# A fixed order on three engines up to the second cell of a fused attention and two-layer kernel

## Chip, cores and metric

The kernel runs on one core of a Trainium2 chip. The metric is the device time of one execution in microseconds (us). The engines are TensorE (PE, matrix products into PSUM), VectorE (DVE), ScalarE (ACT), GpSimd (POOL) and SyncE (SP, whose queue issues all the DMAs here). Each engine works through its own queue in order and waits on the others by semaphores.

## What is computed

A Nyström attention over 4 batches of 8 heads (sequence 576, head size 64, 32 landmarks) feeds two layers, one multiplicative and one with a mish activation. Cut to what matters:

```python
q_lm, k_lm = (mean over 18 neighbours of q, of k)       # 32 landmarks per head
A, Bm, C = sm(q, k_lm), sm(q_lm, k_lm), sm(q_lm, k)     # sm: softmax of the scaled scores
Z = Bm.T / (norms of Bm)
for _ in range(6):
    Z = 2 * Z - Z @ Bm @ Z
x = A @ Z @ C @ v                                       # 2304 tokens x 512
x = ((x @ w_a) * (x @ w_b)) @ w_out                     # width 1536
h = x @ w_in2
out = (h * tanh(softplus(h))) @ w_out2                  # width 2048
```

## The kernel before, in words

All products of the two layers run as three products of rounded halves (a high part and the rest, fp32r), and the fp32 weights first go through a bitwise conversion: `to_f32` (L310) is one ACT instruction (L317) and four DVE instructions on a 128x512 piece (L320, L323, L324, L325). The weights of the first layer come in 36 such units (`Units`, L336): for each of three parts of the width there are eight units for w_a and w_b (two groups of four, which land in a tile `wab`) and four for w_out (`wo1_unit`, which also splits the piece into high and rest, tile `wo`).

Attention runs per batch, in steps of `attention` (L118): `kl`, `ql` sum keys and queries to landmarks; `sB`, `BB` make the small score matrix and its start for the inverse; six `NS` steps iterate the inverse (tile `rz`), each a PE step of small matmuls, then an ACT copy and a DVE add; the last also makes `zd`; `sC0`, `sC1` are the scores of all keys (tile `E`), `ET0`, `ET1` their transposes, `U` the product with the values, `M` joins U and the inverse (tile `mt`); `A0`, `A1` score the two halves of the queries and `A0n`, `A1n` normalise them (tile `at`, a high part from ACT and the rest from POOL, L288).

The first layer is cut into 12 **cells** of (batch, part of the width), and each cell into 8 **slots**. `emit_bm` (L404) folds M into the first layer's weights (a **fold**, two per cell: PE matmuls `ps_bm<-wab,mt`, ACT high part, DVE rest, tile `bm`). A slot (`emit_ab`, L430) is twelve matmuls `ps_ab<-at,bm` in two halves, an ACT copy `ta`, a DVE product `tg` (L437), an ACT high part and a POOL rest (tile `g`, 9 buffers). `emit_o1` (L447) is the product with w_out: 8 **o1** pieces per cell, each twelve matmuls `ps_o<-g,wo` over four `g` tiles and four `wo` tiles.

The order: PE and ACT instructions written through `Written` (L37) stay in the order of the code until L603; those of DVE are placed by a scheduler, except a few that are pinned. Up to there the code is a string of steps of batch 0 (L593), with `u` for a whole conversion unit and digits for warming matmuls on the identity. After that the 96 slots run in a loop (L634); work that has a due time in slots lies in a list `todo` (L617): the steps of batch 1 between slots 0.5 and 5.5, four w_out units from slot 2, the second part's twelve units from slot 6 to 18, and so on; and each slot emits one waiting o1 piece between its halves (`between`, L652), two in slots 7 and 8. From L603 on the scheduler orders PE and ACT too.

Of the kernel before, what the change touches and what calls it, by code (L numbers as in the profile page):

```python
# [17 lines left out]
LM = 32  # L18
# [13 lines left out]
def nystrom_moe_kernel(ctx: ExitStack, tc: tile.TileContext, q, k, v, w_a, w_b, w_out1, w_in2, w_out2, out):  # L32
    nc = tc.nc
    NT = B * S
    ve, gp = nc.vector, nc.gpsimd

    class Written:  # L37
# [7 lines left out]
        def __getattr__(self, name):  # L45
            f = getattr(self.engine, name)

            def call(*a, **kw):
                i = f(*a, **kw)  # L49
                if Written.on:  # L50
                    tc.keep_in_program_order(i)
                return i

            return call

    ac, pe = Written(nc.scalar), Written(nc.tensor)
# [8 lines left out]
    ps = ctx.enter_context(tc.tile_pool(name="ps", bufs=1, space=PSUM))  # L65

    def bank(tag):
        return ps.tile([128, 512], F32, tag=tag, bufs=2, name=f"ps_{tag}")

    def pair_bank(tag):  # L70
        return ps.tile([128, 2, 512], F32, tag=tag, bufs=1, name=f"ps_{tag}")
# [22 lines left out]
    def load_qk(ap, b):  # L94
        out = []
        for src, nm, tag in ((k, "kt", "kv"), (q, "qt", "qt")):
            t = ap.tile([128, 4, S], F32, tag=tag, bufs=1, name=nm)
            nc.sync.dma_start(out=t.rearrange("p j s -> p (j s)"), in_=src[b])
# [18 lines left out]

    def attention(ap, b, kt, qt, vt0=None):  # L118
# [3 lines left out]
        wheel = [0]  # L122
# [4 lines left out]
        def pair():  # L127
            wheel[0] += 1
            return pair_bank("bm" if first and wheel[0] % 2 else "at")

        def lm_sum(src, nm):
            x[nm] = sm([128, 4, LM], nm)
            for j in range(0, 4, 2):
# [15 lines left out]
        def sB():  # L149
            p = pair()  # L150
            tile4(p, lambda o, rows, j: (o[:, 0:32], x["ql"][rows, j, :], x["kl"][rows, j, :]))
            st = x["st"] = sm([128, 2, 8], "stB")
# [3 lines left out]
            ac.activation(eb, eb, AF.Exp, scale=SC_B)  # L156
            ve.tensor_reduce(out=st[:, :, 2], in_=eb, axis=AX, op=ALU.add)
# [7 lines left out]
        def BB():  # L165

            st, bc = x["st"], x["bc"]
            p = pair()
            for c in range(2):
# [3 lines left out]
                for h in range(4):  # L173
                    r = slice(32 * h, 32 * h + 32)
                    pe.matmul(p[r, c, 64:96], bc[r, c, 1], bc[r, c, 1], start=True, stop=True)
            ve.tensor_reduce(out=st[:, :, 0:2], in_=p[:, :, 0:64].rearrange("p c (a l) -> p c a l", a=2), axis=AX, op=ALU.max)
# [10 lines left out]
        def NS():  # L187
# [4 lines left out]
            p = pair()  # L192
            nx = x["rz"] = sm([128, 2, 2, LM], "rz", 2)
            for c in range(2):
                for h in range(4):
# [4 lines left out]
                    )  # L200
            if not lo:
                ac.activation(nx[:, :, 0], p[:, :, 0:32], AF.Copy)
            ve.tensor_tensor(nx[:, :, 1], p[:, :, 32:64], rz[:, :, 1], op=ALU.add)
            if lo:
                zd = x["zd"] = sm([128, 2, 4, LM], "zd")
                for c in range(2):
                    (ve if first else gp).tensor_tensor(zd[:, c], bd3, nx[:, c, 1:2].to_broadcast([128, 4, LM]), op=ALU.mult)

        def sC(r):
            if r == 0:  # L210
                x["sc"], x["pc"] = sm([128, 4, 2], "stC"), []
            sc, p = x["sc"], pair_bank("bm" if r else "at")
            x["pc"].append(p)
            tile4(p, lambda o, rows, j: (o[:, 0:288], x["ql"][rows, j, :], kt[rows, j, 288 * r:288 * r + 288]))
            ve.tensor_reduce(out=sc[:, r], in_=p[:, :, 0:288], axis=AX, op=ALU.max)
            if r == 0:
                return
            ve.tensor_tensor(sc[:, 2], sc[:, 0], sc[:, 1], op=ALU.max)
# [3 lines left out]
            for r, p in enumerate(x.pop("pc")):  # L222
                for c in range(2):
                    ac.activation(E[:, c, 288 * r:288 * r + 288], p[:, c, 0:288], AF.Exp, bias=sc[:, 3, c:c + 1], scale=SC_A)

        def e_T(c):
            if c == 0:
                x["ET"] = sm([128, 2, 5, 128], "ET")
            p = pair()
# [5 lines left out]
            ac.activation(ET[0:64, 4], p[0:64, 1, 0:128], AF.Copy)  # L235

        def Uv():
            p = pair()
            for c in range(2):
                for i in range(5):  # L240
                    r = slice(0, min(128, S - 128 * i))
                    for j in range(4):
# [4 lines left out]
                        if (c, i, j) == (0, 0, 0):  # L247
                            tc.keep_in_program_order(ins)
# [6 lines left out]
        def M():  # L255
            p = pair()
# [145 lines left out]
    bm = {}  # L402
# [466 lines left out]
```

## Time and profile before

| | |
|---|---|
| median of 3 runs | 863.75 us (861.7 to 863.79) |
| the profiled execution's own time | 862.38 us |
| its span | 860.6 us |
| mean granted TensorE clock, share of full speed | 0.969 |
| busy in the span: PE, DVE, ACT, POOL | 94%, 64%, 40%, 18% |
| bytes moved by DMA | 180.87 MB |

A row of a timeline or of the chain of waits starts with the start in us and the length in us. A group of instructions names line, engine, operation, tile written <- tiles read, shapes and a count, then busy time and the mean length in ns. Behind a bar or in brackets stands the idle time before the instructions and who ended it. A PE "busy" includes modelled ends, so a PE that is busy all the time is not necessarily at its peak.

### The profile page before, as it was taken

The numbers are of one execution on the slowest core, as the hardware profiler recorded it, in microseconds if no ns is written. First come the engines' busy times: TensorE is split into PE (matmuls) and PEld (weight loads), VectorE is DVE, ScalarE is ACT, GpSimd is POOL, SyncE is SP. The second block draws the span as 40 slices with busy tenths as digits, with TensorE's granted clock in tenths as the row PEclk, the third lists the DMA queues.
The fourth block names the chain that finished last, engine by engine and source line by source line (L and its number), as shares of the span: only waits on it lengthen the run. The fifth ranks groups of instructions, "written<-read, shape, count | busy, mean of one in ns | idle before, by whom it ended". The sixth has DMA issues, their size and how long they took to land.

```text
span 860.6 us, 14629 instructions
## 1 busy us (share of the span) xinstructions
PE 805.4 (94%) x5830; PEld 696.0 (81%) x5830; DVE 553.3 (64%) x1024; ACT 346.1 (40%) x686; POOL 157.0 (18%) x147
## 2 busy tenths in 40 slices
PE   4767799999999999999898899999999999999998
PEld 3445578887897797887798799898989888998986
DVE  7787868888375379787996667858533347432433
ACT  3234436435332464353444545445323235332332
POOL 0022211222122133121226433521000000000000
PEclk9778699999999999999999999999999999999999
DMA  9532746649543816877576976789755446655502
GB/s 356 239 117 99 254 151 200 226 152 319 197 156 114 308 34 221 292 226 266 175 235 250 346 249 216 269 293 339 296 185 201 158 180 219 212 204 194 184 1 75
DMA packets 47605, 180.87 MB, mean 210 GB/s; under 512 B 4144, under 2 KB 12336, under 8 KB 37936
## 3 DMA queue, kind: packets, MB, share of 16 engines
q1 hardware_dynamic: 47536, 179.93, 58.8%
q8 instruction: 46, 0.75, 0.3%
q14 instruction: 23, 0.19, 0.1%
HBM read 126.44 MB, written 53.48 MB: 209 GB/s over the span
## 4 chain that ended last, share of the span: by engine, by line
PE 79%; DVE 12%; DMA 5%; issue 2%; ACT 1%; POOL 1%; SPq 0%; DVEq 0%; ACTq 0%
PE ps_ab L49 34%; PE ps_o L49 22%; PE ps_bm L49 13%; PE ps_at L49 10%; DVE f L324 1%; DMA wi2d<-f 1%; DVE f L325 1%; DVE f L320 1%; DMA qt<-in_q_dram 1%; DVE tg L437 1%; DMA kt<-in_k_dram 1%; DVE f L323 1%; DMA wo2d<-f 1%; DMA xq<-x2d 1%; DVE ql L138 1%
## 5 line engine op out<-in xcount | busy, mean ns | idle before, releaser
L49 PE MATMUL ps_ab<-xc,wc 128*128 128x384 f32 x1008 | 201.9, 339 | 2.6 <-ACT m L49 2.1
L49 PEld LDWEIGHTS ps_ab<-xc,wc 128*128 128x128 f32 x1008 | 181.6, 189 | 15.1 <-ACT m L49 2.3
L49 PE MATMUL ps_ab<-at,bm 128*128 128x288 f32 x1152 | 187.1, 303 | 6.9 <-DVE tg L437 4.3
L49 PEld LDWEIGHTS ps_ab<-at,bm 128*128 128x128 f32 x1152 | 161.3, 190 | 37.6 <-issue 9.8
L49 PE MATMUL ps_o<-g,wo 128*128 128x288 f32 x1152 | 182.2, 300 | 10.1 <-ACT wo L49 4.3
L49 PEld LDWEIGHTS ps_o<-g,wo 128*128 128x128 f32 x1152 | 162.6, 190 | 23.9 <-issue 7.3
L334 POOL TENSOR_TENSOR g<-tg,g 128x288 fp32r<-128x288 f32 x96 | 88.1, 918 | 283.6 <-ACT g L49 283.6
L49 ACT ACTIVATE m<-c 128x384 f32<-128x384 f32 x96 | 50.4, 525 | 185.5 <-DVE c L759 185.5
L49 PE MATMUL ps_bm<-wo,g 128*128 128x512 f32 x288 | 94.1, 394 | 0.3 <-ACT g L49 0.3
L49 PE MATMUL ps_at<-wo,g 128*128 128x512 f32 x288 | 83.3, 393 | 0.0
L49 PE MATMUL ps_o<-wo,g 128*128 128x512 f32 x288 | 79.4, 393 | 0.0
L49 ACT ACTIVATE g<-tg 128x288 fp32r<-128x288 f32 x96 | 42.6, 444 | 86.7 <-DVE tg L437 86.6
L334 DVE TENSOR_TENSOR g<-m,g 128x384 fp32r<-128x384 f32 x96 | 60.7, 633 | 25.8 <-ACT g L49 25.7
L437 DVE TENSOR_TENSOR tg<-ps_ab,ta 128x288 f32<-128x288 f32 x96 | 43.4, 452 | 30.3 <-PE ps_ab L49 24.3
L49 PEld LDWEIGHTS ps_at<-wo,g 128*128 128x128 f32 x288 | 53.9, 188 | 10.3
L49 PEld LDWEIGHTS ps_o<-wo,g 128*128 128x128 f32 x288 | 53.6, 188 | 8.9
L49 PEld LDWEIGHTS ps_bm<-wo,g 128*128 128x128 f32 x288 | 53.4, 187 | 7.0 <-ACT g L49 0.6
L49 ACT ACTIVATE ta<-ps_ab 128x288 f32<-128x288 f32 x96 | 38.9, 405 | 44.0 <-PE ps_ab L49 43.6
L49 ACT ACTIVATE g<-m 128x384 fp32r<-128x384 f32 x96 | 50.6, 527 | 2.9
L759 DVE TENSOR_TENSOR c<-ps_ab,m 128x384 f32<-128x384 f32 x24 | 13.4, 557 | 51.8 <-PE ps_ab L49 51.8
L49 PE MATMUL ps_bm<-wab,mt 64*32 64x512 f32 x384 | 42.2, 636 | 1.2 <-ACT mt L49 0.7
L759 DVE TENSOR_TENSOR u2s<-ps_ab,m 128x384 f32<-128x384 f32 x24 | 13.4, 557 | 44.6 <-PE ps_ab L49 44.2
(144 smaller groups left out, 832.8 us busy)
## 6 DMA issues: line engine op xcount, KB each, us to landing
wc<-wcd SPq DMA_DIRECT2D x16, 1792.0 KB, 7.3
wo<-wod SPq DMA_DIRECT2D x16, 1024.0 KB, 4.8
stg<-in_moe_w_out_dram SPq DMA_DIRECT2D x28, 512.0 KB, 4.5
wcd<-wc SPq DMA_DIRECT2D x8, 1792.0 KB, 7.2
wab<-wabd SPq DMA_DIRECT2D x10, 1024.0 KB, 6.5
stg<-in_moe_w_in_dram SPq DMA_DIRECT2D x16, 512.0 KB, 4.9
wod<-wo SPq DMA_DIRECT2D x8, 1024.0 KB, 6.5
stg<-in_moe_w_a_dram SPq DMA_DIRECT2D x12, 512.0 KB, 5.5
```

What stands on the lines that cost most here:

```text
L49: i = f(*a, **kw)
L138: i = ve.tensor_reduce(out=x[nm][:, j:j + 2], in_=src[:, j:j + 2].rearrange("p j (t k) -> p j t k", k=BLK), axis=AX, op=ALU.add,)
L320: i = ve.tensor_scalar(dst, dst, F32_TINY, F32_HUGE, op0=ALU.max, op1=ALU.min)
L323: ve.tensor_scalar(du, du, 3, 0x3FFFFFFF, op0=ALU.logical_shift_left, op1=ALU.bitwise_and)
L324: ve.scalar_tensor_tensor(du, hi, 0xC0000000, du, op0=ALU.bitwise_and, op1=ALU.bitwise_or)
L325: ve.scalar_tensor_tensor(du, lo, 29, du, op0=ALU.logical_shift_right, op1=ALU.bitwise_or)
L334: lo_eng.tensor_tensor(dst_lo, src, dst_hi.bitcast(F32), op=ALU.subtract)
L437: ve.tensor_tensor(tg, pb[:, 0:288], ta, op=ALU.mult)
L759: ve.tensor_tensor(t, p[:, 0:TB], other, op=ALU.add)
```

## The change

All three engines get a written order up to the end of the first cell. The VectorE handle is wrapped like those of ScalarE and TensorE (`ve = Written(nc.vector)`). Every attention step and every conversion becomes a generator that yields at its handovers, and two strings, `FIRST` (batch 0) and `SECOND` (cell (0, 0) with batch 1, marked +), place the pieces one by one; a "." is one piece of a conversion. The DVE work of conversion units 5 to 8, which the scheduler had put ahead of the first fold's rest, moves into `SECOND`. All eight slots of cell (0, 0) stand in `SECOND`; all eight o1 pieces of that cell are deferred: they start after slot 9, and slots 10 to 17 emit two pieces each. `A1` and `A1n` of batch 1 and the four w_out units come at slots 8 to 10, the second part's units at slots 10 to 18. The first three `g` tiles get buffers of their own (12 in all), `qt` gets two buffers, so that batch 1's queries load at the start; batch 0's keys and queries load in halves. PSUM is laid out in a first pool with a third pair of banks (`p3`). The rest of the first `at` tile of batch 0 and `zd` of batch 1 move from POOL to DVE. The warming matmuls in the string go from 25 to 17.

```diff
-    ve, gp = nc.vector, nc.gpsimd
+    gp = nc.gpsimd
...
-    ac, pe = Written(nc.scalar), Written(nc.tensor)
+    ac, pe, ve = Written(nc.scalar), Written(nc.tensor), Written(nc.vector)
...
+        out, step = [], 4 if b else 2
+        for src, nm, tag, bufs in ((k, "kt", "kv", 1), (q, "qt", "qt", 2)):
+            t = ap.tile([128, 4, S], F32, tag=tag, bufs=bufs, name=nm)
+            for j in range(0, 4, step):
+                nc.sync.dma_start(out=t[:, j:j + step].rearrange("p j s -> p (j s)"), in_=src[b][:, S * j:S * (j + step)])
...
+    PAIRS0 = {"sC0": "p3", "ET0": "bm", "ET1": "p3", "A0": "bm", "U": "p3"}
+    PAIRS1 = {"ET0": "bm", "ET1": "bm"}
...
-                    (ve if first else gp).tensor_tensor(zd[:, c], bd3, nx[:, c, 1:2].to_broadcast([128, 4, LM]), op=ALU.mult)
+                    (ve if b < 2 else gp).tensor_tensor(zd[:, c], bd3, nx[:, c, 1:2].to_broadcast([128, 4, LM]), op=ALU.mult)
...
-            gp.tensor_tensor(at[:, 1], af, at[:, 0].bitcast(F32), op=ALU.subtract)
+            (ve if (b, r) == (0, 0) else gp).tensor_tensor(at[:, 1], af, at[:, 0].bitcast(F32), op=ALU.subtract)
...
+    FIRST = """
+        kl kl ql ql . sB sC0 sC1 4 sB . sB BB 3 sC0 BB NS 2 . NS NS 2 . NS NS 2 sC1 NS NS 2 sC1 . sC1 NS NS 1 . sC1 NS NS 1 . NS
+        ET0 ET1 . . U A0 . . A0 . . U A0 M . . . . f0 A1 A0n A0n A0n f0
+    """
+    SECOND = """
+        s0 s0 A1 A1 s0 s1 s1 +kl A1n A1n s1 A1n +kl s2 s2 +ql s2 +ql s3 s3 +sC0 . s3 +sC0 +sC1 . +sC1 +sC1 +sC1 +sC1
+        +sB . +sB . . +sB +BB . . +BB +NS . +NS +NS . +NS +NS . +NS +ET0 +NS . . +NS +ET1 +NS . . +NS +NS . . +NS
+        f1 +U f1 s4 s4 +U +M F s4 s5 s5 F +A0 s5 s6 s6 +A0 +A0 s6 s7 s7 +A0n +A0n s7 +A0n
+    """
...
+        if gpool is None:
+            t = p1.tile([128, 2, 288], F32R, tag="g", bufs=9, name="g1")
+        else:
+            t = gpool.tile([128, 2, 288], F32R, tag="gx", bufs=3, name="g1")
...
-    u0.prefetch()
-    run0 = attention(ap, 0, kt, qt, load_v(ap, 0))
+    u0.prefetch(4)
+    vt0 = load_v(ap, 0)
+    u0.prefetch(8)
+    run0 = attention(ap, 0, kt, qt, vt0)
+    run1 = attention(ap, 1, *load_qk(ap, 1))
+    u0.prefetch(10)
...
-    for e in 'kl ql sB sC0 sC1 u 7 BB 8 NS ET0 1 NS ET1 u NS 2 A0 NS u 2 A0n NS U u 3 NS 2 M u'.split():
...
+    part["."] = weights()
+    part["f0"] = fold(0, 0)
+    go(FIRST, run0)
...
+    part["f1"], part["F"] = fold(0, 1), fold(1, 0)
+    for n in range(8):
+        part[f"s{n}"] = ab(0, n // 4, n // 2 % 2, n % 2, ap if n < 3 else None)
+    go(SECOND, run0)
     Written.on = False
...
-    for w, t0, t1 in ((1, 6, 18), (2, 18, 34)):
+    for w, t0, t1 in ((1, 10, 18), (2, 18, 34)):
...
-        todo.append((2 + 0.9 * n, 99, u0.step))
+        todo.append((8 + 0.5 * n, 99, u0.step))
...
-            if o1q:
+            if o1q and si > 9:
                 emit_o1(*o1q[0], i)
                 if i == 1:
                     o1q.pop(0)
-            if si in (7, 8) and i == 1:
-                for part in range(2):
-                    emit_o1(*o1q[0], part)
+            if si in range(10, 18) and i == 1:
+                for h in range(2):
+                    emit_o1(*o1q[0], h)
                 o1q.pop(0)
```

Three places of the resulting order. VectorE, batch 0, around the start of the `NS` steps: `rz` is the iterate, `wab` a conversion of w_a and w_b, `stC` the maximum of the key scores. Before:

```order
L182 TENSOR_TENSOR rz<-ps_at,stB 128x2x32
L184 TENSOR_TENSOR rz<-bc,stB 128x2x32
L324 SCALAR_TENSOR_TENSOR wab<-stg,wab 128x2x256
L320 TENSOR_SCALAR wab<-wab 128x2x256
L325 SCALAR_TENSOR_TENSOR wab<-stg,wab 128x2x256
L183 TENSOR_TENSOR rz<-ist,rz 128x2x32
L325 SCALAR_TENSOR_TENSOR wab<-stg,wab 128x2x256
L320 TENSOR_SCALAR wab<-wab 128x2x256
L323 TENSOR_SCALAR wab<-wab 128x2x256
L320 TENSOR_SCALAR wab<-wab 128x2x256
L203 TENSOR_TENSOR rz<-ps_bm,rz 128x2x32
```

After:

```order
L56 TENSOR_TENSOR rz<-ps_at,stB 128x2x32
L56 TENSOR_TENSOR rz<-ist,rz 128x2x32
L56 TENSOR_TENSOR rz<-bc,stB 128x2x32
L56 TENSOR_SCALAR wab<-wab 128x2x256
L56 TENSOR_TENSOR rz<-ps_at,rz 128x2x32
L56 SCALAR_TENSOR_TENSOR wab<-stg,wab 128x2x256
L56 TENSOR_TENSOR rz<-ps_at,rz 128x2x32
L56 TENSOR_REDUCE stC<-ps_bm 128x2
L56 TENSOR_TENSOR rz<-ps_at,rz 128x2x32
L56 TENSOR_TENSOR stC<-stC 128x2
L56 TENSOR_SCALAR stC<-stC 128x2
L56 SCALAR_TENSOR_TENSOR wab<-stg,wab 128x2x256
```

Between two steps of `rz` stand up to eight conversion instructions before and about one now.

TensorE, from cell (0, 0)'s first slots into batch 1's attention (`ps_ab<-at,bm` are slots, 12 matmuls each; the small ones are steps sB, sC, BB). Before:

```order
L49 MATMUL ps_ab<-at,bm 128x288 x24
L49 MATMUL ps_at<-kl,ql 32x32 x2
L49 MATMUL ps_bm<-kt,ql 32x288 x2
L49 MATMUL ps_at<-kl,ql 32x32 x6
L49 MATMUL ps_bm<-kt,ql 32x288 x6
L49 MATMUL ps_at<-kt,ql 32x288 x8
L49 MATMUL ps_ab<-at,bm 128x288 x12
L49 MATMUL ps_at<-bc,ones 32x64 x4
L49 MATMUL ps_at<-bc 32x32 x4
L49 MATMUL ps_at<-bc,ones 32x64 x4
L49 MATMUL ps_at<-bc 32x32 x4
L49 MATMUL ps_bm<-wab,mt 32x512 x8
```

After:

```order
L56 MATMUL ps_ab<-at,bm 128x288 x48
L56 MATMUL ps_at<-kt,ql 32x288 x8
L56 MATMUL ps_bm<-kt,ql 32x288 x8
L56 MATMUL ps_at<-kl,ql 32x32 x8
L56 MATMUL ps_at<-bc,ones 32x64 x4
L56 MATMUL ps_at<-bc 32x32 x4
L56 MATMUL ps_at<-bc,ones 32x64 x4
L56 MATMUL ps_at<-bc 32x32 x4
L56 MATMUL ps_at<-rz 32x64 x24
L56 MATMUL ps_bm<-ident,E 128x128 x4
```

Four slots now stand in a row, and batch 1's steps follow without a slot between them.

TensorE, around the o1 pieces that need the fourth w_out tile (`wo_947` before, `wo_1104` after; these two are the same tile). Before:

```order
L49 MATMUL ps_bm<-wab,mt 32x512 x8
L49 MATMUL ps_o_1036<-g_1004,wo_947 128x288 x2
L49 MATMUL ps_o_1079<-g_1004,wo_947 128x288 x2
L49 MATMUL ps_o_1036<-g_1004,wo_947 128x288
L49 MATMUL ps_o_1079<-g_1004,wo_947 128x288
L49 MATMUL ps_ab<-at,bm 128x288 x4
L49 MATMUL ps_o_1105<-g_564,wo_705 128x288 x3
```

After:

```order
L56 MATMUL ps_o_1131<-g_894,wo_1080 128x288
L56 MATMUL ps_o_1165<-g_894,wo_1080 128x288
L56 MATMUL ps_ab<-at,bm 128x288 x6
L56 MATMUL ps_o_1131<-g_926,wo_1104 128x288 x2
L56 MATMUL ps_o_1165<-g_926,wo_1104 128x288 x2
L56 MATMUL ps_o_1131<-g_926,wo_1104 128x288
L56 MATMUL ps_o_1165<-g_926,wo_1104 128x288
L56 MATMUL ps_ab<-at,bm 128x288 x7
L56 MATMUL ps_o_1195<-g_533,wo_998 128x288 x3
```

The place comes after 8 slots and three folds before, and after 15 slots and four folds now.

## Rows read from the trace of the kernel before

**Rows 1.** The page: the span, and busy time of each engine.
```profile
span 860.6 us, 14629 instructions
...
PE 805.4 (94%) x5830; PEld 696.0 (81%) x5830; DVE 553.3 (64%) x1024; ACT 346.1 (40%) x686; POOL 157.0 (18%) x147
```

**Rows 2.** Busy time of each engine by stage, with granted clock; columns in the first line.
```profile
core 0: us, PE busy (x) PEld busy (x) DVE busy (x) ACT busy (x) POOL busy (x), PEclk, DMA share, GB/s
0.00:10.00 10.00, 1.21 (x6) 1.24 (x7) 4.16 (x4) 1.28 (x1) 1.33 (x12) 1.00 0.82 309
10.00:30.00 20.00, 13.76 (x182) 10.67 (x181) 19.93 (x55) 9.23 (x20) 0.00 (x0) 0.82 1.04 405
30.00:45.40 15.40, 11.27 (x199) 7.05 (x198) 8.12 (x22) 2.89 (x6) 1.40 (x1) 0.79 0.32 115
45.40:60.00 14.60, 8.88 (x76) 5.42 (x76) 14.29 (x29) 3.12 (x7) 3.53 (x3) 0.78 0.31 112
60.00:78.00 18.00, 16.30 (x194) 12.95 (x193) 11.44 (x27) 10.89 (x27) 5.47 (x6) 0.90 0.27 100
78.00:99.00 21.00, 11.26 (x176) 6.40 (x176) 16.83 (x38) 7.40 (x14) 4.47 (x4) 0.57 0.65 228
...
101.50:156.00 54.50, 54.50 (x398) 43.93 (x397) 41.58 (x69) 27.48 (x59) 9.13 (x10) 1.00 0.56 180
```

**Rows 3.** The chain that ended last, 0 to 170 us: start, length, what.
```profile
0.75 0.38 SPq L98
1.19 7.61 DMA qt<-in_q_dram
8.82 2.61 DVE ql L138 x2
...
44.21 1.23 DVE bm L334
...
104.50 1.02 PE ps_bm L49 x16
...
146.43 1.59 PE ps_ab L49 x12
```

**Rows 4.** Timeline: the last conversion before o1 runs freely, the first free o1, the next slot.
```profile
98.40 0.69 DVE L334 TENSOR_TENSOR wo<-f,wo 128x512 fp32r<-128x512 f32 x1 [1.92 <-ACT wo L49]
...
99.79 1.70 PE L49 MATMUL ps_o<-g,wo 128*128 128x288 f32 x6
```

**Rows 5.** DVE's groups, 0 to 110 us: busy us, mean ns of one, idle before.
```profile
L324 DVE SCALAR_TENSOR_TENSOR wab<-stg,wab 128x512 uint32<-128x512 uint32 x11 | 8.1, 733 | 0.1
...
L334 DVE TENSOR_TENSOR bm<-ps_bm,bm 128x1024 fp32r<-128x1024 f32 x4 | 4.9, 1223 | 6.0 <-ACT bm L49 6.0
...
L437 DVE TENSOR_TENSOR tg<-ps_ab,ta 128x288 f32<-128x288 f32 x9 | 4.1, 453 | 3.0 <-ACT ta L49 2.1 <-PE ps_ab L49 0.9
...
L282 DVE TENSOR_TENSOR sa<-sa,stA 128x576 f32<-128x576 f32 x4 | 3.0, 758 | 0.1
...
L207 DVE TENSOR_TENSOR zd<-bdm,rz 128x128 f32<-128x128 f32 x2 | 0.5, 289 | 0.1
```

**Rows 6.** Timeline: the first NS matmuls, one step's ACT and DVE part, matmuls at lower clock.
```profile
24.12 0.43 PE L49 MATMUL ps_bm<-rz 32*32 32x64 f32 x16 [1.91 <-DVE rz L183]
...
66.15 0.23 ACT L49 ACTIVATE rz<-ps_at 128x64 f32<-128x64 f32 x1 [0.71 <-PE ps_at L49]
...
66.64 0.21 DVE L203 TENSOR_TENSOR rz<-ps_at,rz 128x64 f32<-128x64 f32 x1
...
31.26 0.65 PE L49 MATMUL ps_bm<-rz 32*32 32x64 f32 x16
```

**Rows 7.** Timeline: a fold's ACT part; slots, product U and a fold at the lower clock.
```profile
43.15 1.02 ACT L49 ACTIVATE bm<-ps_bm 128x1024 fp32r<-128x1024 f32 x1 [1.25 <-PE ps_bm L49]
...
58.63 2.77 PE L49 MATMUL ps_ab<-at,bm 128*128 128x288 f32 x10 [0.68 <-POOL at L288]
...
86.84 2.87 PE L49 MATMUL ps_at<-vt,ET 128*32 128x65 f32 x80 [1.62 <-issue]
...
97.90 1.96 PE L49 MATMUL ps_bm<-wab,mt 64*32 64x512 f32 x16 [0.37 <-ACT mt L49]
```

More of the change, by code (lines that the diff above doesn't have):

```diff
@@ L294, in attention, with run @@
         }
-        return lambda name: steps[name]()
+        part = {}
+        def run(name, whole=True):
+            g = part.pop(name, None) or steps[name]()
+            for _ in g:
+                if not whole:
+                    part[name] = g
+                    return
+        return run
+    FIRST = """
[7 more added lines that the diff above has]
+    """
     def stage(src, shape, early):
@@ L413, in emit_bm @@
         t = main.tile([128, 2, 2, 512], F32R, tag="bm", bufs=3, name="bm")
-        split(t[:, 0], t[:, 1], p, ac, ve)
+        ac.activation(t[:, 0], p, AF.Copy)
+        yield
+        ve.tensor_tensor(t[:, 1], p, t[:, 0].bitcast(F32), op=ALU.subtract)
         bm[b, g] = t
+    def emit_bm(b, g):
+        for _ in fold(b, g):
+            pass
     g1 = {}
@@ L590, in fill, with weights, go @@
             pe.matmul(p[:, 0:128], ident, ident, start=True, stop=True)
[L592 to L602 removed]
+    def weights():
+        gs = []
+        for n in range(8):
+            u0.n += 1
+            u0.prefetch()
+            gs.append(u0.units[n][2](u0.st[n]))
+        next(gs[0])
+        yield
+        for n, g in enumerate(gs):
+            for i, _ in enumerate(g):
+                if i == 2 and n < 7:
+                    next(gs[n + 1])
+                yield
+            yield
+    part = {}
+    def go(text, run):
+        for e in text.split():
+            if e.isdigit():
+                fill(int(e))
+            elif e[0] == "+":
+                run1(e[1:], False)
+            elif e in part:
+                next(part[e], None)
+            else:
+                run(e, False)
+    part["."] = weights()
+    part["f0"] = fold(0, 0)
+    go(FIRST, run0)
+    p3 = None
+    ps_ctx.close()
+    ps.append(ctx.enter_context(tc.tile_pool(name="ps", bufs=1, space=PSUM, reuse_waits="tile")))
+    part["f1"], part["F"] = fold(0, 1), fold(1, 0)
+    for n in range(8):
+        part[f"s{n}"] = ab(0, n // 4, n // 2 % 2, n % 2, ap if n < 3 else None)
+    go(SECOND, run0)
     Written.on = False
[L604 to L605 removed]
     CELLS = [(b, w) for w in range(3) for b in range(2)] + [(2, 0), (2, 1), (3, 0), (3, 1), (2, 2), (3, 2)]
```

144 lines of the change are left out of this document (78 added, 66 removed).

## The prediction, made before the changed kernel ran

> **What bounds the kernel now.** I read the page first: over the 860.6 us PE is busy for 94% and DVE for 64% [rows 1], so the end of the kernel is set by PE, and a change of order can only gain where PE lacks work. The stages show where that is [rows 2]. From 101.5 to 156 us PE is busy for all 54.5 us. Ahead of that it is not: the clock falls to 0.57 of full speed between 78 and 99 us, and PE's records there are stretched. In these first 99 us DVE is the engine with the work: 19.93 us of 20 between 10 and 30, 14.29 of 14.60 between 45.4 and 60, 16.83 of 21 between 78 and 99; in all 4.16 + 19.93 + 8.12 + 14.29 + 11.44 + 16.83 = 74.8 us busy and 24.2 idle. The chain of waits says the same in its first part: queries from DMA, the landmark sums on DVE, later the rest of the first fold, which ends at 45.4 us [rows 3]. PE becomes free of DVE when the fourth w_out tile is split, at 98.40 + 0.69 = 99.1 us, and the last o1 matmuls that needed it end at 99.79 + 1.70 = 101.5 us [rows 4]. So I ask how much PE work is done when DVE has finished that same tile in the new order, and when that is.
>
> **PE's side of the comparison.** In the new order the place behind the fourth w_out tile comes after 15 slots and 4 folds; before, after 8 slots and 3 folds; the o1 matmuls done are the same 24. Seven slots at 1.59 us and one fold at 1.02 [rows 3] are 12.1 us of dense PE work. The old kernel, dense from 101.5 on, has done as much at 101.5 + 12.1 = 113.6 us. Everything that lets the new order reach the place before 113.6 us is gain; PE's work behind it is the same.
>
> **DVE's work up to there.** Removed: nothing. Added ahead of the place: six products tg at 0.453, two rests of folds at 1.223; moved from POOL: one rest of at (128x576; no row on DVE, by the nearest of that shape, sa, 0.758) and two zd at 0.289, which overlap to 0.5 [rows 5]. That is 2.7 + 2.4 + 0.8 + 0.5 = 6.4 us on the 74.8, or 81.2 us. So DVE has more to do, not less; the gain must come from this work doing PE more good, and from less idle time. The new order by itself I walked with the durations of the groups, each stage's sum times 0.92, because neighbouring instructions overlap: along the old order the durations of all the groups of that view add up to 81.1 us, and the stages show 74.8 [rows 2].
>
> Start: the keys and queries come in halves. Before, the queries land at 8.8 us and their sums end at 11.4 [rows 3]. With halves each sum runs behind its own half, and only the last, 1.3 us, is left after 8.8: 10.1 us. Two more issues on SP's queue, 0.38 us each [rows 3], come ahead of the weights, behind the sums of the keys; I cost them at nothing, and uncovered they would cost 0.8.
>
> 10.1 to 23.1: sB, BB, six NS. Before, the first NS matmul started at 24.1 us [rows 6], because up to eight conversion instructions stood between the small ones. Now it starts at 15.0. One NS step is PE 0.43 us, ACT 0.23, and DVE 0.21 after ACT [rows 6], with handovers 1.12 us; at the lower clock PE takes 0.65 and the step 1.34. A conversion piece (at most 0.73 [rows 5]) fits in the 0.9 us in which DVE waits for the next step. Six steps with one delay of 0.7, where ACT makes E first, end at 22.6, zd at 23.1. DVE is busy 8.9 of these 13 us.
>
> 23.1 to 40.9: transposes, U, A0, M, first fold. Here DVE waits for ACT to copy the transposes before it may convert unit three (1.5 us), for the scores A0 behind U on PE (1.3), and at the end for ACT's high part of at. Busy 12.5 of 17.8. The rest of the first fold ends at 40.9, against 45.4 [rows 3]: 4.5 us earlier, but with four conversions fewer behind it, about 8 us of DVE work that is still to come.
>
> 40.9 to 71: four slots while DVE sums batch 1's landmarks, then batch 1's sC, sB, BB and NS with units five to eight between. Busy 25.6 of 30.1; the idle time is a wait for POOL's rest of the second at (1.3), for ACT's E ahead of a conversion (0.9), and for NS steps. No slot is left to fill PE here: PE idles, which costs nothing as long as DVE is the bound, but lets the clock fall.
>
> 71 to 86.5: the second fold, U, a slot, M, the third fold, a slot, A0, in one line. Each fold is PE, then ACT's 1.02 us, then DVE's 1.22, with PE and DVE in turn waiting. At the lower clock a fold takes 1.96 instead of 1.02, U 2.87, twelve slot matmuls 1.2 x 2.77 = 3.3 instead of 1.59 [rows 7]. Busy only 8.1 of 15.5. This is the weakest stretch of the new order: what is queued on DVE behind the wait for a fold (two tg, the transposes of A0) is needed by PE two steps later.
>
> 86.5 to 106.9: A0n, A1, A1n of batch 1, four w_out units, seven tg; nothing to wait for, PE works ahead on slots. Busy 20.4. With 0.8 for the o1 matmuls behind, the place is reached at 107.6 us.
>
> **The sum.** 113.6 - 107.6 = 6.0 us gained. DVE's total: 5.6 + 8.9 + 12.5 + 25.6 + 8.1 + 20.4 = 81.1 us, as counted above, and 25.8 idle, against 24.2 before. So what pays is not less waiting but that PE's seven slots are done inside the stage that DVE bounds.
>
> **Behind the place.** The second part's twelve units fall in slots 10 to 18 instead of 6 to 18, but the doubled o1 pieces stretch these slots: from the place to slot 18 PE has 33.6 us of work, DVE 29. Before, in the 54.5 us to 156, DVE was busy for 41.6 [rows 2]. So PE stays the bound, by little; I take the frictions as equal to before's (about 4 us over that stretch) and keep 0 to 5 us as the cost if DVE's pieces come late for a fold. Buffers: tg of slot 15 waits for a g buffer that the first deferred o1 pieces free, at about 111 us, when DVE has conversions to do until 112: nothing. The loads behind batch 1's values on SP's queue wait for that tile until U, near 74 us; what they bring is first needed near 95: nothing.
>
> The profiled run's own time is 862.38 us, 1.4 under the median of 863.75. From the profile: 862.38 - 6.0 = 856.4; against the median, 857.7. I give **857.5**.
>
> **Bounds.** The idle time is the unknown. If DVE packs its instructions as it did between 10 and 30 us, where 19.93 of 20 us were busy with interleaved pieces, the factor is nearer 0.82 than 0.92 (87.6 us of durations: 72 busy) and the place comes near 98: 848. If every handover from 23 to 86.5 takes half as much idle time again (17.3 becomes 26) it comes at 116: 866.
>
> **Rivals.**
> *More gain, 843 to 852.* The packing just named, together with less idle time. For it: the stretch from 10 to 30. Against it: the new order puts small dependent steps between the pieces.
>
> *No change, 861 to 866: the clock.* The granted clock was 0.57 between 78 and 99 us although slots were strewn among the steps [rows 2]. The new order leaves PE with batch 1's small steps alone from 52 to 71 us, and has 17 warming matmuls instead of 25. If PE stands at the lower of its two levels (1.2 of 2.4 GHz) from 13 us to the third fold, twelve NS steps cost 0.22 each, three folds 0.9, two products U 0.5, and four slots 1.7: 2.6 + 2.7 + 1.0 + 6.8 = 13.1 us at most; I have half of it in the walk, the other half takes the gain: 857.7 + 6.5 = 864. The Trainium skill, "TensorE: Matmul & The Clock Gate", Part 1, says that the lower rate is the default and that only activity lifts it; by that rule the 8 warming matmuls taken out work against this change.
>
> *Slower, 866 to 872: DVE's queue in `SECOND`.* DVE was free to take what was ready, now it stands behind each wait. Before, an unready fold let a conversion pass; now the queue behind it (tg, sa, the next fold's rest) waits too, and PE, whose two ab banks are freed by tg, with it. The trace has 6.0 us of waiting for ACT ahead of four rests of folds [rows 5]. If the walk's idle time from 40.9 to 86.5, 12 us, doubles, the place is reached at 119.6, 6.0 later than before: 870. It decides at 113.6 us. The Trainium skill, same page, "Architectural detail", calls ScalarE's and VectorE's queues strict first-in first-out; the order of rows here is kept on each engine, so the trace agrees.
>
> *The order isn't realised.* The scheduler still orders everything behind `SECOND`; but the new order shows the o1 pieces and all slots where the text puts them, so I give this nothing of its own.
>
> **How the numbers follow.** Forecast, 852 to 861: 0.46. More gain, below 852: 0.20. No change, 861 to 866: 0.19. Slower, above 866: 0.15. The range 848 to 868 leaves out some 0.1 at the lower and 0.1 at the upper end. Faster by over 0.3% (2.6 us, about what a measurement of this kernel can tell from no change) is all of the first two: 0.66. Within 0.3%: 0.18 of the third. Slower by over 0.3%: 0.16.
>
> **What would show it.** In the profile after: the rest of the first fold ends at 41 us (38 to 43), batch 1's zd at 71, the fourth w_out tile at 107 (98 to 116), 15 slots done by then; PE dense from there on. DVE's idle time up to that tile should be 25 us, and its largest waits those for ACT and PE at the folds between 71 and 86.5. The forecast is wrong if the tile comes later than 113, if the granted clock up to 86 us is below 0.6 throughout, or if PE waits for DVE's folds between 107 and 145 us by more than 5 us.

## The result, and the profile after

The changed kernel is slower: 870.99 us median of 4 runs (868.94 to 871.91) against 863.77 beside it, ratio 1.0074, 95% interval 1.0053 to 1.0096. The forecast was 857.5, faster. The profiled execution's span is 869.3 us against 860.6 [rows 1], 8.7 us more. Its page, same rows:

```profile
span 869.3 us, 14596 instructions
...
PE 809.5 (93%) x5814; PEld 698.5 (80%) x5814; DVE 560.3 (64%) x1027; ACT 345.2 (40%) x686; POOL 152.6 (18%) x144
```

The stages of [rows 2] in the changed kernel; columns as there:

```profile
0.00:10.00 10.00, 2.60 (x12) 2.63 (x12) 5.64 (x5) 1.28 (x1) 1.33 (x12) 1.00 0.83 315
10.00:30.00 20.00, 14.53 (x322) 9.90 (x320) 14.42 (x47) 6.75 (x18) 0.00 (x0) 0.98 1.03 405
30.00:45.40 15.40, 9.77 (x58) 5.85 (x56) 14.13 (x26) 5.26 (x10) 0.80 (x1) 0.69 0.49 185
45.40:60.00 14.60, 7.65 (x72) 6.34 (x72) 10.04 (x19) 5.38 (x13) 3.80 (x4) 0.76 0.26 91
60.00:78.00 18.00, 12.77 (x250) 8.18 (x250) 11.30 (x36) 4.39 (x12) 0.00 (x0) 0.72 0.24 79
78.00:99.00 21.00, 15.41 (x126) 10.61 (x124) 16.12 (x30) 9.17 (x18) 6.22 (x7) 0.84 0.26 97
```

DVE is busier early in attention, and the clock between 78 and 99 us is 0.84 instead of 0.57. But between 60 and 78 us PE has 12.8 us of work instead of 16.3: the slots that filled it before are done. Three rows of DVE's timeline (start, length) are the marks of the prediction: the first fold's rest, zd of batch 1, the split of the fourth w_out tile.

```profile
37.40 1.22 DVE L56 TENSOR_TENSOR bm<-ps_bm,bm 128x1024 fp32r<-128x1024 f32 x1
...
72.76 0.49 DVE L56 TENSOR_TENSOR zd<-bdm,rz 128x128 f32<-128x128 f32 x2
...
112.08 0.69 DVE L56 TENSOR_TENSOR wo<-f,wo 128x512 fp32r<-128x512 f32 x1 [0.33 <-ACT wo L56]
```

38.6 us (forecast 40.9), 73.3 (71), and 112.8 (106.9). With 0.8 us for the o1 matmuls behind, the equal-work place comes at 113.6 us, where the old kernel has it: up to there both traces have 203 matmuls of slots and o1 pieces and 64 of folds. The forecast gain of 6.0 us is therefore not there.

A lead comes behind that place, and goes again. The products tg of slot 18, then of slot 24; each pair is before, then after:

```profile
155.34 0.45 DVE L437 TENSOR_TENSOR tg<-ps_ab,ta 128x288 f32<-128x288 f32 x1
```
```profile
149.40 0.45 DVE L56 TENSOR_TENSOR tg<-ps_ab,ta 128x288 f32<-128x288 f32 x1
```
```profile
175.26 0.46 DVE L437 TENSOR_TENSOR tg<-ps_ab,ta 128x288 f32<-128x288 f32 x1 [3.06 <-ACT bm L49]
```
```profile
175.22 0.46 DVE L56 TENSOR_TENSOR tg<-ps_ab,ta 128x288 f32<-128x288 f32 x1 [4.49 <-PE ps_ab L56]
```

At slot 18 the new kernel is 5.9 us ahead, with 9 o1 matmuls and 16 of a fold less behind it. At the prediction's prices these are 2.2 us, so 3.7 us are a true lead. At slot 24 nothing of it is left. PE's rows show one thing that goes with this, the price of a fold in pieces (changed kernel; a fold's matmuls, then what PE does next):

```profile
159.15 1.09 PE L56 MATMUL ps_bm<-wab,mt 64*32 64x512 f32 x16
160.17 1.86 PE L56 MATMUL ps_ab<-at,bm 128*128 128x288 f32 x12
...
173.04 1.04 PE L56 MATMUL ps_bm<-wab,mt 64*32 64x512 f32 x2
174.01 1.06 PE L56 MATMUL ps_ab<-at,bm 128*128 128x288 f32 x6
```

The next matmuls start 1.02 us behind the start of all 16 of a fold, and 0.97 us behind the start of 2 of them. A visit of PE to a fold thus costs about 1 us, however few of its matmuls are done in it, and the scheduler cuts folds into several visits. From 113.6 us to slot 18 there are 9 visits before and 5 after; from there to slot 24, 3 and 6. These differences, 4 and 3 us, are near the lead and its loss; no run changes the visits alone.

To see the rest, cut the run at two more products tg, those of slot 56 (where the conversions of the second layer's weights begin) and of slot 95 (the last):

```profile
314.03 0.46 DVE L437 TENSOR_TENSOR tg<-ps_ab,ta 128x288 f32<-128x288 f32 x1 [0.17 <-PE ps_ab L49]
```
```profile
313.66 0.45 DVE L56 TENSOR_TENSOR tg<-ps_ab,ta 128x288 f32<-128x288 f32 x1
```
```profile
467.31 0.46 DVE L437 TENSOR_TENSOR tg<-ps_ab,ta 128x288 f32<-128x288 f32 x1 [1.93 <-PE ps_ab L49]
```
```profile
473.35 0.46 DVE L56 TENSOR_TENSOR tg<-ps_ab,ta 128x288 f32<-128x288 f32 x1 [1.84 <-POOL g L382]
```

So 0.3 us is gained up to slot 56; the **weight stage** (slots 56 to 95) takes 159.7 us instead of 153.3, 6.4 lost; the rest takes 395.9 instead of 393.3, 2.6 lost. The diff changes nothing in what these two parts do; only the PSUM pool that they use is opened anew, with another setting for the waits on its buffers (a_f3 and b_f3, below, differ in it too and take the same time). In both kernels the scheduler orders them, though, and the two PE orders differ up to the start of the second layer. The weight stage of before, then of after:

```profile
314.03:467.31 153.28, 145.78 (x1154) 127.44 (x1154) 130.51 (x233) 69.30 (x143) 46.23 (x46) 1.00 0.67 225
```
```profile
313.66:473.35 159.69, 149.86 (x1169) 133.29 (x1168) 129.57 (x234) 69.74 (x143) 46.31 (x46) 0.97 0.64 211
```

PE is idle for 2.3 us more and busy for 4.1 more. It does 14 o1 matmuls more in the stage, some 1.9 us, which the old kernel does elsewhere, mostly behind slot 95; for equal work the stage loses some 4.5 us. The clock is enough for that: by the trace's clock record PE stands at the lower of its two levels (1.2 of 2.4 GHz) for 10.2 us of the stage after and never before, and at half rate that costs at most 5.1 us. Each of the three falls follows a short wait (PE is busy for 0.51 of the 2 us ahead of the second, 0.80 of 2 ahead of the third). At the first, PE does 0.90 us of work in 3 us and then runs slowly:

```profile
358.00:361.00 3.00, 0.90 (x4) 0.46 (x3) 1.23 (x2) 2.15 (x4) 1.24 (x1) 0.89 0.95 370
361.00:364.00 3.00, 3.00 (x14) 3.00 (x15) 2.51 (x6) 1.01 (x3) 0.49 (x1) 0.55 0.05 18
```

One wait, without a fall behind it, in the chain that ended last (start, length, what):

```profile
411.39 0.44 DVE tg L56
411.83 6.80 DMA wi2d<-f
...
418.65 0.69 ACT f L361
...
419.37 0.44 DVE f L365
...
423.66 0.07 DVE tg L56
```

A converted piece f goes back to DRAM (wi2d<-f, issued behind the loads xq of the second layer); its buffer, one of two, is free 6.8 us later; ACT starts the next piece in it; and in DVE's queue the piece stands ahead of tg, for which PE waits.

### The profile page after: what moved, and what is told of

It reads as the page before. It is cut to its first block, busy times and chain, and to the rows that moved or that the text cites. A ratio compares the mean times of both kernels' runs of the same rounds, so it can differ in the third digit from the quotient of the medians.

```text
span 869.3 us, 14596 instructions
## 1 busy us (share of the span) xinstructions
PE 809.5 (93%) x5814; PEld 698.5 (80%) x5814; DVE 560.3 (64%) x1027; ACT 345.2 (40%) x686; POOL 152.6 (18%) x144
## 4 chain that ended last, share of the span: by engine, by line
PE 74%; DVE 11%; DMA 8%; issue 3%; ACT 3%; POOL 0%; SPq 0%; DVEq 0%; ACTq 0%
PE ps_ab L56 32%; PE ps_o L56 19%; PE ps_bm L56 12%; PE ps_at L56 10%; DVE f L56 2%; DMA wi2d<-f 2%; DVE wab L56 1%; DMA stg<-in_moe_w_a_dram 1%; DVE tg L56 1%; DVE sa L56 1%; DMA xq<-x2d 1%; DMA wo2d<-f 1%; DMA stg<-in_moe_w_out_dram 1%; DVE f L365 1%; DVE bm L56 1%
## 5 line engine op out<-in xcount | busy, mean ns | idle before, releaser
L56 PE MATMUL ps_ab<-at,bm 128*128 128x288 f32 x1152 | 195.1, 310 | 19.8 <-ACT at L56 8.1
L56 PEld LDWEIGHTS ps_ab<-at,bm 128*128 128x128 f32 x1152 | 167.4, 196 | 49.2 <-ACT at L56 9.5
L56 DVE TENSOR_TENSOR g<-m,g 128x384 fp32r<-128x384 f32 x96 | 66.2, 690 | 23.6 <-ACT g L56 23.6
L56 DVE SCALAR_TENSOR_TENSOR f<-stg,f 128x512 uint32<-128x512 uint32 x88 | 68.2, 777 | 1.3
L56 PE MATMUL ps_bm<-wab,mt 64*32 64x512 f32 x384 | 44.9, 620 | 2.1 <-ACT mt L56 2.1
```

## Experiments

Theory A: the first part is no worse; the loss comes from the order that the scheduler makes of the weight stage. Theory B: the new first part leaves a debt. The last four columns are us, from the one profiled execution of each kernel: tg of slot 56, slots 56 to 95, how much of that PE stood at its lower clock, and from slot 95 to the end. The ratio is to the kernel before as measured beside each run (medians of 862.4 to 863.8).

| kernel | median us | ratio to before, 95% | to slot 56 | weight stage | at the lower clock | rest |
|---|---|---|---|---|---|---|
| before | 863.8 | | 314.0 | 153.3 | 0 | 393.3 |
| after | 871.0 | 1.0053 to 1.0096 | 313.7 | 159.7 | 10.2 | 395.9 |
| b_pin56 | 867.7 | 1.0036 to 1.0082 | 313.5 | 159.3 | 10.2 | 393.2 |
| a_pin56 | 872.6 | 1.0087 to 1.0140 | 314.3 | 161.6 | 17.1 | 395.6 |
| f_pin56 | 874.4 | 1.0110 to 1.0155 | 317.1 | 159.8 | 10.2 | 394.5 |
| b_shift | 872.0 | 1.0075 to 1.0123 | 315.1 | 157.8 | 6.8 | 396.7 |
| a_s3 | 866.5 | 1.0019 to 1.0050 | 316.4 | 153.2 | 3.4 | 394.5 |
| b_nc56 | 849.3 | 0.9827 to 0.9856 | 312.7 | 141.7 | 0 | 392.1 |
| a_nc56 | 853.9 | 0.9879 to 0.9912 | 314.2 | 142.1 | 0 | 395.2 |
| b_f3 | 859.7 | 0.9935 to 0.9988 | 313.8 | 149.3 | 0 | 394.9 |
| a_f3 | 859.8 | 0.9939 to 0.9981 | 314.8 | 149.3 | 0 | 395.1 |
| a_g8 | 869.6 | 1.0049 to 1.0098 | 314.8 | 158.6 | 10.2 | 395.1 |
| a_spread | 868.6 | 1.0042 to 1.0083 | 314.4 | 150.6 | 3.4 | 401.7 |
| b_spread | 873.5 | 1.0088 to 1.0146 | 313.0 | 154.8 | 3.4 | 404.2 |
| a_f3s | 870.7 | 1.0054 to 1.0114 | 314.8 | 154.1 | 0 | 400.6 |
| a_wo | 869.9 | 1.0043 to 1.0094 | 315.2 | 157.5 | 6.8 | 395.5 |
| a_warm | 873.4 | 1.0087 to 1.0137 | 323.2 | 154.0 | 3.4 | 395.4 |
| a_port | 871.8 | 1.0058 to 1.0131 | 316.7 | 157.0 | 3.4 | 397.8 |

One comparison stands in the table by itself. The changed kernel, a_port, a_wo and a_warm have the same PE order from slot 57 to slot 95, matmul for matmul. Their weight stages take 159.7, 157.0, 157.5 and 154.0 us, and the longest has the most time at the lower clock. Less half of that time they take 152.3 to 155.3 us; the stage before takes 153.3. So the same order loses the clock more often in one execution than in another, and the split of one trace is uncertain by some us.

**The order pinned.** In the loop, in both kernels (PE and ACT only, up to slot 95):

```diff
+        if si == 56:
+            Written.on = True
```

> The kernel before, with TensorE and ScalarE kept in the order of the code from slot 56 to the last slot (VectorE as before). It is one half of a pair: with the same pin on the changed kernel, the two have the same TensorE order from slot 56 on and differ only ahead of it. Theory A (the changed kernel's first part is no worse, its loss comes from the other order that the scheduler makes of the second layer's weight stage): the pin itself may cost some us on the kernel before, 862 to 872, and matters only as the base of the pair. Theory B (the new first part itself leaves a debt of 7 us): the same for this half; the difference of the pair decides.

> The changed kernel with the same pin from slot 56 on. Theory A: 1 to 5 us faster than the kernel before with that pin, since the trace of the changed kernel has slots 47 to 63 some 1 to 5 us ahead for the TensorE work done, and the loss of 12 us comes behind slot 63. Theory B: some 7 us slower than the kernel before with that pin, as without it.

The pair differs by 5.0 us; theory A wanted a gain of 1 to 5, B a loss of 7. Up to slot 92 the two are level (tg at 460.8 and 460.7 us). Then, after the same wait of 2.0 us, the clock falls in one and not in the other (the next slot's matmuls; b_pin56, then a_pin56; idle time in brackets):

```profile
460.84 1.05 PE L49 MATMUL ps_ab<-at,bm 128*128 128x288 f32 x6 [2.03 <-ACT ta L49]
```
```profile
460.74 1.48 PE L56 MATMUL ps_ab<-at,bm 128*128 128x288 f32 x6 [2.00 <-ACT ta L56]
```

That costs 3.0 us by slot 95; 2.3 follow at the start of the second layer. Neither theory has it: the first part is level, as A says, but an equal order of PE does not give an equal time. The pin also costs the old kernel 5 us (867.7 against 862.4 beside it), and its weight stage is 6.1 us longer, with 10.2 us at the lower clock.

**The first string alone.** The string `FIRST`, then the old loop, with the same pin:

```diff
-    go(SECOND, run0)
+    run0("A1")
+    Written.on = False
+    run0("A1n")
+    for _ in part["."]:
+        pass
```

> Only the first string of the changed kernel (batch 0 in pieces, halves of the first loads, batch 1's queries early), then the loop of the kernel before: batch 1 between slots 0.5 and 5.5, w_out units from slot 2, no deferred o1; pinned from slot 56 as the other two. Theory A1 (the gain of 6.8 us at the first fold survives where the rest is left to the scheduler): 4 to 6 us faster than the kernel before with the pin, and 1 to 4 us faster than the changed one with the pin. Theory A2 (what the first string gains, VectorE's work behind it takes back, because the conversions moved behind the fold come due later): within 2 us of the kernel before with the pin.

6.7 us slower than b_pin56. The tg of slot 0 comes at 42.3 us instead of 48.2, that of slot 8 at 112.6 instead of 108.6. That the conversions which the string moved behind the first fold come due in between is argued, not tried. A1 falls, and A2 with it, which wanted no loss.

**One number, before and after.**

```diff
-    ... ((1, 0.5, 5.5), (2, 27, 40), (3, 41, 55.9)):
+    ... ((1, 0.5, 5.5), (2, 26, 40), (3, 41, 55.9)):
```

> The kernel before with one number changed: the steps of batch 2 are due between slots 26 and 40 instead of 27 and 40. Nothing ahead of slot 24 moves; behind it the scheduler makes another order up to the end of the slots, among others with the loads xq of the second layer 7 places earlier on SP's queue, where the changed kernel has them too. Theory A (the order of the later stage is worth several us whatever sets it off): 2 to 9 us slower than the kernel before. Theory B: within 1.5 us of it.

9.5 us slower than the kernel before beside it, with nothing changed ahead of slot 24, and just past theory A's range. Its profile runs 2.3 us late at slot 8 already, where the program is the same, which is what executions differ by, and level again at slot 24; 4.5 is in the weight stage, 3.4 in the rest. The other way round, in the changed kernel, `(3, 41, 55.9)` became `(3, 40, 55.9)`:

> The changed kernel with one number changed: the steps of batch 3 are due from slot 40 instead of 41. Up to slot 30 nothing moves; from there to slot 90 the scheduler makes another order. Theory A (the loss behind slot 64 is a matter of which order the scheduler happens to make, not of the new first part): a time that differs from the changed kernel's by more than 2 us, on either side, 862 to 879. Theory B (the loss comes from the first part): 869.5 to 872.5.

4.5 us faster than the changed kernel. Its weight stage takes 153.2 us, 6.5 less, as in the kernel before. Both medians moved as theory A has it: an order that the scheduler happens to make there is worth as much as the whole result. How much of each stage's change is the order and how much the clock of that one execution, a single trace can't tell.

**Without the conversions' VectorE work.** With the pin:

```diff
-        yield from to_f32(f, st)
+        held(ac.engine.activation(f, st[:, :, 1].bitcast(F32), AF.Abs))
+        yield
```

> The kernel before with the pin from slot 56 on, and without the four VectorE instructions of each conversion of the second layer's weights (32 units; only the ScalarE instruction and the DMA back to DRAM are left, so that the second layer is computed with other weights): 32 x 2.2 = 70 us of VectorE work are gone from slots 56 to 88. Base of a pair. Theory A (the changed kernel loses its time in that stage, where short waits of TensorE for VectorE and ScalarE pull the granted clock down): with the waits gone, 845 to 858 us. Theory B (the loss is the first part's): the same for this half.

> The changed kernel with the same pin and the same conversions left out. Theory A: within 2 us of the kernel before with these edits, because the first parts are equal at slots 34 to 64 of the traces (difference 0 to 1 us) and the stage where 9 us are lost has no stalls left. Theory B: 5 us slower, as the pinned pair with its conversions was.

The weight stage shrinks to 142 us in both, against 159.3 and 161.6 with the pin alone: the conversions cost 18 and 19 us there. Without them the clock doesn't fall in the stage. The pair still differs by 4.7 us: theory A, which wanted at most 2, misses, and B named 5. But most of the difference doesn't come out of the first part: 1.4 us are there up to slot 56, 0.4 in the stage and 3.1 in the rest, which the conversions don't touch.

**A third buffer for f.** Room for it comes from one g buffer:

```diff
-        f = base.tile([128, 512], F32, tag="f24", bufs=2, name="f24")
+        f = base.tile([128, 512], F32, tag="f24", bufs=3, name="f24")
...
-            t = p1.tile([128, 2, 288], F32R, tag="g", bufs=9, name="g1")
+            t = p1.tile([128, 2, 288], F32R, tag="g", bufs=8, name="g1")
```

> The kernel before with three buffers instead of two for the converted piece f of the second layer's weights, and 8 instead of 9 g buffers to make room. Theory A' (in the weight stage each conversion waits for the DMA of the piece two before it, up to 4.3 us, and VectorE's queue stands behind it, so that TensorE stalls and its clock falls): less TensorE idle time between slots 56 and 95, 856 to 863 us. Theory A'' (the stalls come from VectorE's load and the order alone): 861 to 872, as any new order of that stage.

> The changed kernel with the same two edits. Theory A': some 5 to 10 us faster than the changed kernel, 860 to 866. Theory A'': 865 to 875.

> The changed kernel with 8 instead of 9 g buffers and nothing else: the other half of the pair of edits that made it 11 us faster. Theory A' (the third buffer for f gave the gain): 868 to 874. Rival (the new order that any edit sets off gave it): below 866.

859.7 and 859.8 us: both are faster than the kernel before, as theory A' has it, and the change is worth nothing between them. Here the two have the same PE order in the weight stage without a pin. The g buffer alone does nothing for the changed kernel (869.6); it was not tried on the kernel before. What ACT waits for between 314 and 475 us (total, times, longest), in the changed kernel and then with the third buffer:

```profile
ACT f L361 <- DMA wi2d<-f: 17.7, 10, 3.5
ACT f L361 <- DMA wo2d<-f: 6.5, 4, 3.5
```
```profile
ACT f L361 <- DMA stg<-in_moe_w_out_dram: 5.5, 4, 1.8
ACT f L361 <- DMA stg<-in_moe_w_in_dram: 5.4, 4, 2.6
```

The 24.2 us of waiting for f to land are gone, PE waits in the stage for 1.8 us in all instead of 9.6, its clock doesn't fall, and the stage takes 149.3 us in both. This wait is no difference between the two kernels, though: the kernel before has 24.5 us of it in a stage of 153.3 us, and a_s3 33.1 in one of 153.2. It is what the third buffer takes from both. Of 146 us from 314 on, PE is busy for 137.9 in the changed kernel, 143.7 with the buffer:

```profile
314.00:460.00 146.00, 137.94 (x1093) 121.94 (x1091) 119.45 (x216) 63.99 (x132) 36.95 (x40) 0.98 0.67 220
```
```profile
314.00:460.00 146.00, 143.72 (x1130) 124.51 (x1129) 128.63 (x231) 67.27 (x140) 42.57 (x44) 1.00 0.68 231
```

**The conversions at a lower rate.**

```diff
-            u2.step(min(32, si - 56) - u2.n)
+            u2.step(min(32, (si - 56) * 27 // 32) - u2.n)
```

> The changed kernel with the 32 conversions of the second layer's weights strewn over 38 slots instead of 32 (27 in 32 slots). Theory A' (the stage of slots 56 to 95 takes 153 to 161 us instead of 142 because the conversions come as fast as two f buffers, ScalarE and VectorE can just follow): slots 56 to 95 take 148 to 154 us, the run 860 to 866. Rival (the order alone, not the rate): anything from 863 to 875 with that stage at 155 to 160.

> The kernel before with the same edit. Theory A': 857 to 863, and within 3 us of the changed kernel with that edit, since the first parts are equal. Theory B (the new first part leaves a debt of 7 us that does not depend on that stage): 5 to 9 us faster than the changed kernel with it.

> The changed kernel with both: the third f buffer (with 8 g buffers) and the conversions over 38 slots. If the two edits take away the same stalls, as theory A' says: 857 to 861, no more than 3 us below the third buffer alone. If they are two causes: 852 to 856.

The stage does as expected in the changed kernel (150.6 us), but the rest grows by 5 to 11 us in all three: the second layer's first products now wait 8.3 to 8.8 us for ACT's part of their weight tile wc. All three run times miss what was expected of them, and the pair has the opposite sign of the other pairs (the changed kernel is faster by 4.9). So the rate is no remedy, and buffer and rate are not told apart by it.

**The first part.** Three runs ask what sets it. Without the VectorE work of the first w_out units:

```diff
-        yield from to_f32(f, st)
+        if skip:
+            held(ac.engine.activation(f, st[:, :, 1].bitcast(F32), AF.Abs))
```

> The changed kernel without the four VectorE instructions (0.41 + 0.41 + 0.68 + 0.68 us) in each of the first four w_out units (their values are then wrong; the ScalarE instruction, the split and the DMA stay). The order behind slot 18 is the same as in the changed kernel, word for word. Theory D (VectorE's work sets when the fourth w_out tile is split, as the prediction's walk had it, only mis-sized): that split ends some 8 us earlier, at 104 to 106 us instead of 112.8, and the whole run is 5 to 9 us faster, 862 to 866. Rival W (the waits for ScalarE, GpSimd and the second at tile of batch 1 set it): the split moves by less than 4 us, the run by less than 3: 868 to 871.

The split ends at 108.2 us, 4.6 earlier, between D and W; the run, 869.9 us, is W's, and slots 18 and 56 come at 149.1 and 315.2 us, no earlier. Up to 113.6 us DVE is busy for 6.4 us less and PE for the same 75 (after, then this kernel):

```profile
0.00:113.60 113.60, 75.07 (x917) 54.92 (x918) 85.62 (x182) 40.66 (x88) 16.50 (x27) 0.85 0.53 194
```
```profile
0.00:113.60 113.60, 75.24 (x913) 55.53 (x914) 79.18 (x170) 41.19 (x90) 15.80 (x27) 0.82 0.55 204
```

So less work on DVE up to that tile did not let PE do more. PE's order between slots 8 and 18 is another one here, however (the tg of slot 15 comes at 133.2 us instead of 120.7), so the two are not told apart. Then the warming matmuls, `+NS 3` for each `+NS`:

> The changed kernel with 36 warming matmuls more, three behind each NS piece of batch 1; nothing else moves on any engine. Rival C (the low clock between 46 and 76 us takes the gain): the granted clock of 60 to 78 us rises from 0.72 to 0.9 or more, batch 1's zd comes 1.5 to 3 us earlier than at 72.8 us, and the run is 1.5 to 4 us faster, 867 to 869.5. Theory D (VectorE sets it): zd and the fourth w_out split stay within 1 us, the run 870 to 872.

The granted clock of 60 to 78 us rises to 0.80, but zd comes at 76.8 us instead of 72.8: the fillers lie in PE's queue ahead of the small products that the chain needs. The first part grows by 9.5 us, the run by only 2.4, for the weight stage takes 154.0, with 3.4 us at the lower clock. Both theories miss; rival C falls as far as this cure goes. Last, the rest of the first w_out2 tile on VectorE (`ve if k == 0 else gp`):

> The changed kernel with one instruction moved from GpSimd to VectorE: the rest of the first w_out2 tile at the start of the second layer. All orders are the same otherwise. In the changed kernel's trace the sum of the weight tile s on VectorE takes 2.56 us there instead of 0.42 while GpSimd works on that rest (484.1 to 486.7 us), and TensorE waits 3.1 us for u2s behind it. Theory P (the two engines get in each other's way, and that is 3 of the 8.7 us lost): s takes 0.42 us, the wait for u2s is below 1 us, and the run is 2 to 4 us faster, 867 to 869. Rival: the wait only goes to the next instruction (the s_out load, ScalarE's high part): 870 to 872.

The sum takes 0.42 us and the wait for u2s falls to 0.9, but ACT, which waits for the load s_out, has g late instead, and PE waits 3.8 us for that: the rival's case, 871.8 us.

This wait for u2s is also where the rest differs. PE waits 3.1 us for it in the changed kernel, in a_pin56 and in a_nc56, and 0.5, 0.2 and 0.2 us in their partners, whose rest is 2.3 to 3.1 us shorter. In the f3 pair, whose rest is equal, PE waits 0.6 us for it in a_f3.

## Why the prediction was wrong, step by step

- *Up to 86.5 us* the walk held at its ends, in part by luck: the first fold came 2.3 us earlier than forecast, zd 2.3 later, the third fold's rest at 87.6 against 86.5. The stretch to zd took 34.6 us instead of 30.1, the one behind it 14.3 instead of 15.5.
- *"86.5 to 106.9: ... nothing to wait for ... Busy 20.4"* took 25.2 us from 87.6 on. Up to the split DVE was busy for 85.1 us, not 81.2, and idle for 27.7, not 25.8; together 5.8, all of the forecast gain. The mis-sized term is DVE's work in the new order: the added work at 6.4 us, and the overlap, taken from the old order. By one count of all DVE's instructions up to that split the durations add up to 85.0 us before and 92.6 after, 7.7 more, and DVE is busy for 74.9 and 85.1 of them, 0.88 and 0.92 (the prediction has 81.1 for the first sum). The 33 instructions on the tile wab, the same in both kernels, cost DVE 16.46 us before and 18.11 in the new order, where they stand between dependent steps (all instructions of the tile up to that split; DVE is the third time):

```profile
0.00:99.10 99.10, 4.12 (x48) 0.64 (x48) 16.46 (x33) 6.69 (x10) 0.79 0.57 214
```
```profile
0.00:112.80 112.80, 7.57 (x64) 1.08 (x64) 18.11 (x33) 6.12 (x10) 0.85 0.52 194
```

- *"Everything that lets the new order reach the place before 113.6 us is gain"* was not tested by the change, since the place came at 113.6. a_wo speaks against it, with another order on the way: 4.6 us at that split were worth nothing at slot 18.
- *"PE's work behind it is the same"* is the step that gave the wrong sign. The work is the same, its time is not: 9.0 us were lost behind slot 56, in the weight stage, by its trace, mostly to the clock, in the rest to the wait for u2s. I had priced friction only up to slot 18, at 0 to 5 us, and read a PE busy for 94% as a PE at its limit. "Dense from 101.5 on" fails already there: up to the tg of slot 18 PE does 46 us of matmuls, at the prediction's prices, in 53.8 us. The 1.02 us for a fold is the price of a visit, and the old order makes up to five visits to a fold. The weight stage of the kernel before takes 153.3 us with PE shown busy for 138.5 of the 146 us from 314 on, and 141.7 without the conversions' VectorE work (with the pin). The Trainium skill, "Perfetto Trace Analysis", section "Identifying the Most-Contended Engine", says that matmul busy time is a poor measure of how close TensorE is to its limit; this trace agrees, with those two numbers.
- *The rival "slower"* named a time near the measured one, 870, by luck, and the point from which it decides, 113.6, is what was reached. Its mechanism was not what cost the time: the folds between 71 and 87 us came within 2 us of the walk.
- *The rival "no change: the clock"* looked at the clock in the wrong place. The clock up to 113.6 us was better than before (0.85, against 0.80); it fell at 360, 401 and 463 us.
- *"The order isn't realised"* was given nothing, though its own sentence said that the scheduler orders everything behind `SECOND`. That the later parts would be ordered anew was the rival to price.

**Shown:** the first part gains nothing at slot 56 (its tg starts at 312.7 to 314.0 us in before and the three kernels that differ from it only from there on, and at 313.7 to 316.7 in after and its four, on average 1.3 later); the loss lies behind it, in parts whose code is unchanged; it goes with 10.2 us at the lower clock in the weight stage and with the wait for u2s in the rest; an edit of one number moves the time by 4.5 us one way or 9.5 the other; with a third f buffer the two kernels are equal and faster than before. **Open:** what decides whether the clock falls behind a short wait, so whether the old order would lose it as often, which one trace of it doesn't show; whether the fold visits alone make and take the lead at slot 18; and why the rest is shorter in the changed kernel of the spread pair.

## What to carry to other kernels

Where a scheduler orders what lies behind an edit, compare both orders to the end, and cut both traces at the same piece of work further on before the gain is counted. Before forecasting a few us, change one number that should do nothing: what that moves is the size of what can't be forecast, here up to 9 us. Before a stage is explained from one trace, look for another run with the same order in it: here the same order took 154.0 to 159.7 us. A stage in which a queue stands behind a DMA's landing is worth a buffer first: the third f buffer gave 3 us to one kernel and 11 to the other, more than the new order.

## What the runs showed of the hardware

A visit of PE to a fold costs 0.97 us with 2 of its matmuls and 1.02 with 16, in the rows above. The runs don't show why.

A short wait of PE costs more than itself at one time and not at another: the same 2.0 us at 460 us left the clock alone in b_pin56 and brought it down in a_pin56 (1.05 and 1.48 us for the same six matmuls). The runs don't show why.

DVE and GpSimd can stand in each other's way. In the changed kernel GpSimd's rest of wo started 0.3 us ahead of DVE's sum s (start, length):

```profile
484.11 2.61 POOL L382 TENSOR_TENSOR wo<-s_out,wo 128x1024 fp32r<-128x1024 f32 x1 [8.94 <-DMA wcd<-wc]
```
```profile
484.43 2.56 DVE L56 TENSOR_TENSOR s<-s_in 128x256 f32<-128x256 f32 x1
```

The sum took 2.56 us and ended 0.3 us behind the rest. In the kernel before it started 0.07 us ahead of that rest:

```profile
479.59 0.42 DVE L504 TENSOR_TENSOR s<-s_in 128x256 f32<-128x256 f32 x1
```
```profile
479.66 2.59 POOL L334 TENSOR_TENSOR wo<-s_out,wo 128x1024 fp32r<-128x1024 f32 x1 [10.31 <-ACT wo L49]
```

The Trainium skill, "SBUF — State Buffer", section "SBUF: two separate sides", says that a VectorE instruction with two SBUF inputs and a GpSimd instruction that reads SBUF take one port pair for a whole instruction, whichever starts first. The changed kernel's case agrees; in the kernel before the rest, which came second, shows no delay (2.59 against 2.61 us), so this side is not shown. In a_port, with that rest on DVE, the sum takes 0.42 us again.
